# The head of a fused FNet and gMLP kernel: the first DFT block in row halves, hh straight from x

## The chip, the cores and the metric

The kernel runs on one core of a Trainium2 chip, in float32 (matmul operands in float32r). The metric is the device time of one execution in microseconds (us). The core's engines work side by side, each through its own queue in order: TensorE (PE, with its weight loads as PEld), VectorE (DVE), ScalarE (ACT), GpSimd (POOL), and SyncE (SP), which here issues transfers.

## The reference

```python
def _layernorm(x, axis=-1, eps=1e-5):
    m = jnp.mean(x, axis=axis, keepdims=True)
    v = jnp.var(x, axis=axis, keepdims=True)
    return (x - m) / jnp.sqrt(v + eps)

def _A_ref(x, dft_seq_re, dft_seq_im, dft_hid_re, dft_hid_im):
    a = jnp.einsum("bsd,ed->bse", x, dft_hid_re)
    b = jnp.einsum("bsd,ed->bse", x, dft_hid_im)
    return jnp.einsum("ts,bse->bte", dft_seq_re, a) - jnp.einsum("ts,bse->bte", dft_seq_im, b)

x = A_x                                       # (1, 2048, 512)
mod = (_silu(c) @ w_mod).reshape(1, 6, 1, -1)
sa, ca, ga, sb, cb, gb = (mod[:, i] for i in range(6))
h = _layernorm(x) * (1 + ca) + sa
x = x + ga * _A_ref(h, dft_seq_re, dft_seq_im, dft_hid_re, dft_hid_im)
h = _layernorm(x) * (1 + cb) + sb
x = x + gb * _B_ref(h, w_in, w_sp, b_sp, w_out)   # gMLP: GELU, layernorm, a 2048x2048 product, w_out
```

Only the first layernorm and the first product along the sequence, with the 2048x2048 matrices dft_seq_re and dft_seq_im, bear on this change.

## The kernel before

The kernel is one program written out in order. Its first part multiplies the normalized x with the DFT matrices of the sequence. The 2048 rows of x are cut into 16 tiles of 128 rows (s = 0 to 15), the matrices into blocks of 512x512. A step n is one tile s against 128 columns of one block: four of them make a block (k = 0 to 3), steps 0 to 3 are the block of dft_seq_re at the top left, steps 4 to 7 that of dft_seq_im.

Products keep float32 accuracy by splitting each operand: a high part (hh of the normalized tile, ah of the block, rounded to float32r by a copy on ScalarE) and a low part, the remainder (hl and al, a subtraction on VectorE). A step is then three groups of four matmuls, hh with ah, hh with al, hl with ah, one matmul for each quarter of the 512 hidden columns. In steps 0 to 3 (mm_a, n below 4) the three groups are issued one after the other, so that each needs its operands only when its turn comes.

A block arrives in `stage`, a tile of 128 partitions by 16 by 128: partition 32a + j holds the columns 128a to 128a + 127 of the rows 32b + j, b from 0 to 15. To feed a step, VectorE transposes it in squares of 32x32 (`squares`, "the turn"): turn k takes 32 columns of each group a, and all rows. load_block issues four transfers, one for each a. For block 0 it was called twice, on 64 of the 128 columns each time (`s0` to `s1`), so that the turns k = 0 and 1 need the first half, 2 and 3 the second.

The tiles of x: stats_first (rows 0 and 1) and stats_x (later ones) take mean and variance on VectorE and make scale and shift on POOL; norm_x writes the normalized tile xn on ScalarE, its column 0 being set to 1 by a memset (DFT's first hidden column is dealt with elsewhere); hi_h copies xn to hh, lo_h subtracts. prep_hi(n) turns and copies (t, ah), prep_lo(n) subtracts (al).

Order is set by the program's text: each engine runs its instructions in the order in which the calls stand at the end of the function; later work is hung on steps by `at(n, ...)`. Tiles have a fixed number of buffers (`stage` and `t` two, `ah` four, `al` three). The first transfers are issued on SP, those of x's second tile on ScalarE. While data is on its way, keep_busy issues filler matmuls of ones on TensorE:

```python
def keep_busy(n, k):
    ps = bank(k, "busyp")
    for _ in range(n):
        nc.tensor.matmul(ps, ones, busy, start=True, stop=True)
```

Of the kernel before, what the change touches and what calls it, by code (L numbers as in the profile page):

```python
# [8 lines left out]
F32 = mybir.dt.float32  # L9
F32R = mybir.dt.float32r  # L10
AF = mybir.ActivationFunctionType
ALU = mybir.AluOpType

P = 128
# [5 lines left out]
def fnet_gmlp_kernel(  # L20
# [32 lines left out]
    nc = tc.nc  # L53
# [3 lines left out]
    Q = 512  # L57
    NQ = S // Q
    NS = S // P
    ND = D // P  # L60
# [5 lines left out]
    def pool(name, side="left", bufs=1):  # L66
        return tc.tile_pool(name=name, bufs=bufs, side=side, reuse_waits="tile")
# [6 lines left out]
    blocks = ctx.enter_context(pool("blocks"))  # L74
# [4 lines left out]
    def bank(k, name):  # L79
        return psum.tile([P, 512], F32, tag=f"bank{k}", bufs=1, name=name)  # L80
# [30 lines left out]
    def norm(src, name):  # L111

        mean, rstd = stats(src, name)
        nmr = small.tile([P, 1], F32, tag="nmr" + name, name="nmr" + name)
        nc.gpsimd.tensor_scalar(nmr, mean, rstd, -1.0, op0=ALU.mult, op1=ALU.mult)
        return rstd, nmr
# [6 lines left out]
    def at(n, f, *a):  # L123
        fill.setdefault(n, []).append((f, a))
# [9 lines left out]
    src = []  # L134
# [15 lines left out]
    stage, T, AH, AL = {}, {}, {}, {}  # L150

    def load_block(tile_, a, s0=0, s1=P):
        v = a.rearrange("(b j) (a s) -> a j b s", j=32, a=4)
        for q in range(4):
            nc.sync.dma_start(tile_[32 * q:32 * q + 32, :, s0:s1], v[q][:, :, s0:s1])
# [9 lines left out]
    def load(b):  # L165
        if b < len(src):
            stage[b] = blocks.tile([P, 16, P], F32, tag="stage", bufs=2, name=f"stage{b}")
            load_block(stage[b], src[b])
        elif b < len(src) + 2:
            j = b - len(src)  # L170
            XB.append(blocks.tile([P, 4, Q], F32, tag="stage", bufs=2, name=f"xb{j}"))
            for g in range(2):
                nc.sync.dma_start(XB[j][:, 2 * g:2 * g + 2], ht_d[g].rearrange("(k p) t -> p k t", p=P)[:, 2 * j:2 * j + 2])
                for kk in range(2):
                    TT[2 * j + kk, g] = XB[j][:, 2 * g + kk]
        elif 4 * (b - NB0) < NE - N4:
            i, gh = divmod(b - NB0, NQ)
            g, h = divmod(gh, 2)
            p = PROD[i]
            stage[b] = blocks.tile([P, 2, 16, 64], F32, tag="stage", bufs=2, name=f"stage{b}")  # L180
            for r in range(2):
                load_half(stage[b][:, r], s_d[S_OF[p], r, g] if p in S_OF else
                          quad(w_sp, r + (2 if p == 4 else 0), g + (2 if p == 1 else 0)), h)
# [5 lines left out]
    def squares(dst, block, k):  # L189
        nc.vector.transpose(dst.rearrange("p (b i) -> p b i", i=32), block[:, :, 32 * k:32 * k + 32])  # L190
# [10 lines left out]
    def slot(i, name, dtype=F32):  # L201
        return slots[0].tile([P, Q], dtype, tag=f"slot{i}", bufs=1, name=name)
# [33 lines left out]
    def form_t(n):  # L236

        stage1 = n < N3
        p = (YPROD if stage1 else ZPROD)[(n - (N2 if stage1 else N3)) // 4]
        gg, kk = divmod(n % 4, 2)  # L240
        a, b, c, d = TT[kk, gg], TT[2 + kk, gg], TT.get((kk, 2 + gg)), TT.get((2 + kk, 2 + gg))
        if p == 6:
            if stage1:
                S2[gg, kk] = slot(13 + 2 * gg + kk, f"s2_{gg}{kk}")
                nc.vector.tensor_tensor(S2[gg, kk], d, XD[kk] if gg else c, op=ALU.subtract)
            return S2[gg, kk]
        if stage1:
            return {1: a, 2: b, 7: a, 4: b, 5: c, 3: d}[p]
        if p in (1, 2):
            t = blocks.tile([P, Q], F32, tag="t", bufs=2, name=f"t{n}")  # L250
            nc.vector.tensor_tensor(t, a if p == 1 else b, S2[gg, kk], op=ALU.subtract if p == 1 else ALU.add)
            return t
        return {7: c, 4: d, 5: a, 3: b}[p]
# [5 lines left out]
    highs, lows, SE = set(), set(), []  # L259
# [8 lines left out]
    def prep_hi(n):  # L268
        if n >= NE or n in highs:
            return  # L270
        highs.add(n)
        if N2 <= n < N4:
            T[n] = form_t(n)
        else:
            b, k = divmod(n, 4) if n < N2 else (NB0 + (n - N4) // 4, (n - N4) % 4)
            if b != NB0:
                T[n] = blocks.tile([P, Q], F32, tag="t", bufs=2, name=f"t{n}")
            if b == NB0:
                assert n in T
            elif n >= N4:  # L280
                squares(T[n], stage[b][:, k % 2], k // 2)
            else:
                squares(T[n], stage[b], k)
        AH[n] = SE[2][:, n - N4] if N4 <= n < N4 + 4 else blocks.tile([P, Q], F32R, tag="ah", bufs=4, name=f"ah{n}")
        nc.scalar.activation(AH[n], T[n], AF.Copy)  # L285
        if not N2 <= n < N4 and k == 3:
            stage.pop(b)
            if b != NB0:
                load(b + 2)


    def prep_lo(n):
        if n >= NE or n in lows:
            return
        lows.add(n)
        if N2 <= n < N4 and n % 4 == 3:
            AL[n] = slot(0, f"al{n}", F32R) if slots else zrow[0].tile([P, Q], F32R, tag="z1u", bufs=6, name=f"al{n}")
        elif N4 <= n < N4 + 4:
            AL[n] = slot(9 + n - N4, f"al{n}", F32R)
        else:  # L300
            AL[n] = blocks.tile([P, Q], F32R, tag="al", bufs=3, name=f"al{n}")
        t = T.pop(n)
        nc.vector.tensor_tensor(AL[n], t, AH[n].bitcast(F32), op=ALU.subtract)  # L303
        gg, kk = divmod(n % 4, 2)
        if NY[7] <= n < NY[7] + 4:
            nc.vector.tensor_tensor(TT[2 + kk, gg], TT[2 + kk, gg], S2[gg, kk], op=ALU.subtract)
# [6 lines left out]
    spool = s1.enter_context(pool("spool", "right"))  # L313
    GP_ = []
    hp = ctx.enter_context(ExitStack())
    hpool = hp.enter_context(pool("hpool"))
# [4 lines left out]
    ones = cpool.tile([P, P], F32, name="ones")  # L321
# [62 lines left out]
# [5 lines that stand above are left out]
# [14 lines left out]
    X, XG, LN, NRM, h_hi, h_lo = {}, {}, {}, {}, {}, {}  # L403
# [12 lines left out]
    def stats_x(s):  # L416
        NRM[s] = norm([X[s]], "x")

    def stats_first(s):

        m = spool.tile([P, 12], F32, tag="first", bufs=2, name=f"first{s}")
        nc.vector.bn_stats(m[:, :6], X[s])
        mv = m[:, 8:]
        nc.vector.bn_aggr(mv[:, :2], m[:, :6])
        nc.vector.tensor_scalar(mv[:, 1:2], mv[:, 1:2], EPS, None, op0=ALU.add)
        nc.gpsimd.tensor_tensor(mv[:, 2:3], mv[:, 1:2], mhalf, op=ALU.pow)
        nc.gpsimd.tensor_scalar(mv[:, 3:4], mv[:, 0:1], mv[:, 2:3], -1.0, op0=ALU.mult, op1=ALU.mult)
        NRM[s] = mv[:, 2:3], mv[:, 3:4]

    def sum_x(s):  # L430

        LN[s] = spool.tile([P, D], F32, tag="xn", bufs=4, name=f"xn{s}")
        m = NRM[s] = spool.tile([P, 4], F32, tag="sums", bufs=3, name=f"sums{s}")
        nc.scalar.activation(LN[s], X[s], AF.Copy, accum_out=m[:, 0:1])
        nc.gpsimd.tensor_scalar(m[:, 0:1], m[:, 0:1], -1.0 / D, 1.0, op0=ALU.mult, op1=ALU.mult)
# [21 lines left out]
    def hi_h(s):  # L457
        h_hi[s] = hpool.tile([P, ND, P], F32R, name=f"hh{s}")
        nc.scalar.activation(*parts_h(s, h_hi), AF.Copy)

    def lo_h(s):
        h_lo[s] = hpool.tile([P, ND, P], F32R, name=f"hl{s}")
        lo, h = parts_h(s, h_lo)
        nc.vector.tensor_tensor(lo, h, parts_h(s, h_hi)[0].bitcast(F32), op=ALU.subtract)
        LN.pop(s)
# [513 lines left out]
    load_x(0, range(1, 2), nc.scalar)  # L979
    nc.scalar.activation(sc, ones[:, :ND], AF.Silu)  # L980
    stage[0] = blocks.tile([P, 16, P], F32, tag="stage", bufs=2, name="stage0")
    load_block(stage[0], src[0], 0, P // 2)
    load_x(0, range(2, 4))
    load_block(stage[0], src[0], P // 2, P)
    load(1)
    load_x(1, range(2))
    keep_busy(5, 5)
    for s in range(2):
        LN[s] = spool.tile([P, D], F32, tag="xn", bufs=4, name=f"xn{s}")
        nc.gpsimd.memset(LN[s][:, 0:1], 1.0)  # L990
        stats_first(s)
    norm_x(0)
    hi_h(0)
    prep_hi(0)
    norm_x(1)
    lo_h(0)
    prep_lo(0)
    hi_h(1)
    prep_hi(1)
    stats_x(2)  # L1000
    lo_h(1)
    prep_lo(1)
    norm_x(2)
    prep_hi(2)
    stats_x(3)
    hi_h(2)
    norm_x(3)
    at(0, lo_h, 2)
    at(0, hi_h, 3)
    at(1, lo_h, 3)  # L1010
    at(0, load_x, 1, range(2, 4))
    at(2, load_row)
# [7 lines left out]
    for s, n in ((4, 4), (5, 4), (6, 6), (7, 6), (8, 10), (9, 10)):  # L1020
        m = n + (s == 9)
# [295 lines left out]
```

## Time and profile before

| what | us |
|---|---|
| median of three runs (lowest, highest) | 942.41 (942.01, 942.84) |
| the profiled execution | 942.69 |
| its span, first to last instruction | 940.9 |
| busy in the span: TensorE, VectorE, ScalarE, POOL | 932.1, 738.3, 413.6, 195.8 |
| first matmul of step 0 | 9.38 |
| first matmul of step 4 | 21.47 |

Rows of the timeline give start, length, engine, line, operation, output<-input, shapes and, in brackets, how long the engine had stood still and what ended it. Line numbers are those of the kernel before. "SPq" rows are issues of transfers, not their course. Rows of a group give its total and mean length and the idle time ahead of it.

### The profile page before, as it was taken

The page shows a single profiled execution, that of the slowest core. Times are in us where ns is not written, and L with a number is a line of the kernel's source. Part 1 is how long each engine was busy: PE and PEld are TensorE (multiplying, and loading weights), DVE is VectorE, ACT ScalarE, POOL GpSimd, SP SyncE. Part 2 cuts the span into 40 slices and gives each one's busy share as a digit, 9 for nine tenths or more (in the row PEclk, how much of TensorE's full clock was granted, in tenths as well). Part 3 has the DMA queues.
Part 4 walks back from the last instruction along what each step waited for, and adds up shares of the span by engine and source line. Part 5 has one row for each costly group of instructions (what it writes and reads, how often), then busy time and mean ns, then how long its engine had stood idle before and what let it go on. Part 6 is the DMA issues. An engine that isn't in the chain of part 4 may idle for free.

```text
span 940.9 us, 12362 instructions
## 1 busy us (share of the span) xinstructions
PE 932.1 (99%) x4114; PEld 772.7 (82%) x4114; DVE 738.3 (78%) x1201; ACT 413.6 (44%) x726; POOL 195.8 (21%) x372
## 2 busy tenths in 40 slices
PE   9999999999999999999989999999999999999998
PEld 5888888888888888888868999888888888888886
DVE  6899957778677677875888878899799889886662
ACT  4684424232132222222577678675545544331221
POOL 2330000114554165323414211332000000000000
PEclk9999999999999999999999999999999999999999
DMA  9994762647539977994777523344564466743541
GB/s 213 226 235 103 143 146 67 168 134 180 144 87 321 275 212 216 275 332 151 240 264 278 180 95 74 90 100 104 133 142 106 114 145 139 182 110 140 185 173 56
DMA packets 236592, 157.07 MB, mean 167 GB/s; under 512 B 131472, under 2 KB 203408, under 8 KB 236400
## 3 DMA queue, kind: packets, MB, share of 16 engines
q1 hardware_dynamic: 223008, 118.65, 50.5%
q0 software_dynamic: 12128, 37.11, 11.0%
q8 instruction: 32, 0.52, 0.2%
q10 hardware_dynamic: 1392, 0.52, 0.2%
q14 instruction: 32, 0.26, 0.1%
HBM read 119.54 MB, written 36.70 MB: 166 GB/s over the span
## 4 chain that ended last, share of the span: by engine, by line
PE 92%; DVE 2%; DMA 2%; ACT 1%; POOL 1%; issue 1%; SPq 1%; DVEq 0%; ACTq 0%; POOLq 0%
PE gp L95 12%; PE gp L96 12%; PE gp L97 12%; PE gw L97 10%; PE gw L96 10%; PE gw L95 10%; PE op L96 3%; PE op L95 3%; PE op L97 3%; PE yp L97 3%; PE yp L96 3%; PE yp L95 3%; PE z2p L97 2%; PE z2p L95 2%; PE z2p L96 2%; PE z1p L97 1%
## 5 line engine op out<-in xcount | busy, mean ns | idle before, releaser
L285 ACT ACTIVATE ah<-t 128x512 fp32r<-128x512 f32 x244 | 154.1, 632 | 369.7 <-DVE t L190 240.6
L303 DVE TENSOR_TENSOR al<-t,ah 128x512 fp32r<-128x512 f32 x244 | 164.5, 676 | 65.3 <-PE gp L96 38.8
L95 PE MATMUL gp<-ah,hh 128*128 128x512 f32 x496 | 192.9, 389 | 0.0
L96 PE MATMUL gp<-al,hh 128*128 128x512 f32 x496 | 192.9, 389 | 0.0
L97 PE MATMUL gp<-ah,hl 128*128 128x512 f32 x496 | 192.9, 389 | 0.0
L190 DVE STREAM_TRANSPOSE t<-stage 128x512 f32<-128x512 f32 x236 | 165.9, 703 | 6.9 <-DMA stage<-in_A_dft_seq_re_dram 3.0
L96 PE MATMUL gw<-al,bh 128*128 128x512 f32 x400 | 155.6, 389 | 0.0
L97 PE MATMUL gw<-ah,bl 128*128 128x512 f32 x384 | 149.5, 389 | 0.0
L95 PE MATMUL gw<-ah,bh 128*128 128x512 f32 x384 | 149.4, 389 | 0.0
L97 PEld LDWEIGHTS gp<-ah,hl 128*128 128x128 f32 x496 | 93.1, 188 | 19.4
L95 PEld LDWEIGHTS gp<-ah,hh 128*128 128x128 f32 x496 | 93.1, 188 | 19.4
L96 PEld LDWEIGHTS gp<-al,hh 128*128 128x128 f32 x496 | 93.1, 188 | 19.2
L96 PEld LDWEIGHTS gw<-al,bh 128*128 128x128 f32 x400 | 75.1, 188 | 15.7
L97 PEld LDWEIGHTS gw<-ah,bl 128*128 128x128 f32 x384 | 72.1, 188 | 15.0 <-DVE bl L852 0.3
L95 PEld LDWEIGHTS gw<-ah,bh 128*128 128x128 f32 x384 | 72.1, 188 | 15.0
L824 POOL DMA_DIRECT2D s_d<-sj x64 | 35.1, 548 | 103.8 <-DVE sj L816 80.2
L95 PE MATMUL yp<-hth,gh 128*128 128x512 f32 x128 | 49.8, 389 | 0.0
L96 PE MATMUL yp<-htl,gh 128*128 128x512 f32 x128 | 49.8, 389 | 0.0
L97 PE MATMUL yp<-hth,gl 128*128 128x512 f32 x128 | 49.8, 389 | 0.0
L605 POOL DMA_DIRECT2D ht_d<-hturn x62 | 40.9, 665 | 23.6 <-DVE hturn L601 19.6
L95 PE MATMUL op<-woh,uh 128*128 128x512 f32 x112 | 43.6, 389 | 0.0
L96 PE MATMUL op<-wol,uh 128*128 128x512 f32 x112 | 43.6, 389 | 0.0
(220 smaller groups left out, 1466.4 us busy)
## 6 DMA issues: line engine op xcount, KB each, us to landing
stage<-in_A_dft_seq_im_dram SPq DMA_DIRECT2D x64, 256.0 KB, 5.2
sj<-in_B_w_sp_dram SPq DMA_DIRECT2D x32, 512.0 KB, 7.6
s_d<-sj POOLq DMA_DIRECT2D x64, 256.0 KB, 4.1
stage<-s_d SPq DMA_DIRECT2D x128, 128.0 KB, 2.7
stage<-in_A_dft_seq_re_dram SPq DMA_DIRECT2D x60, 256.0 KB, 5.3
stage<-in_B_w_sp_dram SPq DMA_DIRECT2D x88, 128.0 KB, 3.0
wm<-in_w_mod_dram SPq DMA_DIRECT2D x16, 256.0 KB, 5.8
xr<-in_A_x_dram POOLq DMA_DIRECT2D x16, 256.0 KB, 4.6
```

The source lines that it names most:

```text
L95: nc.tensor.matmul(acc, ah, bh, start=first, stop=False, skip_group_check=go_on)
L96: nc.tensor.matmul(acc, ah, bl, start=False, stop=False, skip_group_check=go_on)
L97: nc.tensor.matmul(acc, al, bh, start=False, stop=last, skip_group_check=go_on)
L190: nc.vector.transpose(dst.rearrange("p (b i) -> p b i", i=32), block[:, :, 32 * k:32 * k + 32])
L285: nc.scalar.activation(AH[n], T[n], AF.Copy)
L303: nc.vector.tensor_tensor(AL[n], t, AH[n].bitcast(F32), op=ALU.subtract)
L605: eng.dma_start(v[a, i], ht[32 * a:32 * a + 32].rearrange("c (b r) -> c b r", r=32))
L824: nc.gpsimd.dma_start(s_d[m, r, g][b * P:(b + 1) * P, :], a)
```

## The change

It has three parts.

1. Block 0 is loaded in halves of its rows (load_rows): four transfers for b = 0 to 7, four for b = 8 to 15, each of 128 KB with contiguous runs of 128 floats (before 64 floats). Both halves are issued ahead of the tiles 2 and 3 of x, which had stood between the column halves.
2. Turn 0 and its ah are made in halves (half_first), 256 columns each. The other turns of the block are whole. al of step 0 is subtracted once for both.
3. hh of the tiles 0 to 3 is made straight from x (hi_first): one activation with scale and shift, and one that writes ones into column 0. xn is still made, for hl. All four tiles use stats_first, so `first` gets four buffers. In VectorE's order the second tile's statistics stand behind the first half turn, and xn of each tile behind hh on ScalarE; one filler matmul of five is left out.

```diff
+    def load_rows(j):
+        v = src[0].rearrange("(b j) (a s) -> a j b s", j=32, a=4)
+        for q in range(4):
+            nc.sync.dma_start(stage[0][32 * q:32 * q + 32, 8 * j:8 * j + 8], v[q][:, 8 * j:8 * j + 8])
+
+    def half_first(j):
+        if not j:
+            highs.add(0)
+            T[0] = blocks.tile([P, Q], F32, tag="t", bufs=2, name="t0")
+            AH[0] = blocks.tile([P, Q], F32R, tag="ah", bufs=4, name="ah0")
+        c = slice(Q // 2 * j, Q // 2 * (j + 1))
+        nc.vector.transpose(T[0][:, c].rearrange("p (b i) -> p b i", i=32), stage[0][:, 8 * j:8 * j + 8, :32])
+        nc.scalar.activation(AH[0][:, c], T[0][:, c], AF.Copy)
+
+    def hi_first(s):
+        h_hi[s] = hpool.tile([P, ND, P], F32R, name=f"hh{s}")
+        h = h_hi[s].rearrange("p k (a i) -> p k a i", i=32)
+        nc.scalar.activation(h, X[s].rearrange("p (a k i) -> p k a i", a=4, i=32), AF.Identity,
+                             bias=NRM[s][1], scale=NRM[s][0])
+        nc.scalar.activation(h_hi[s][:, 0, :1], ones[:, :1], AF.Copy)
...
-    load_block(stage[0], src[0], 0, P // 2)
+    load_rows(0)
+    load_rows(1)
     load_x(0, range(2, 4))
-    load_block(stage[0], src[0], P // 2, P)
     load(1)
     load_x(1, range(2))
-    keep_busy(5, 5)
+    keep_busy(4, 5)
...
-        stats_first(s)
+    stats_first(0)
+    half_first(0)
+    hi_first(0)
+    stats_first(1)
+    half_first(1)
+    prep_lo(0)
     norm_x(0)
-    hi_h(0)
-    prep_hi(0)
+    hi_first(1)
+    prep_hi(1)
+    lo_h(0)
+    prep_lo(1)
+    stats_first(2)
     norm_x(1)
-    lo_h(0)
-    prep_lo(0)
-    hi_h(1)
-    prep_hi(1)
-    stats_x(2)
+    prep_hi(2)
     lo_h(1)
-    prep_lo(1)
+    hi_first(2)
     norm_x(2)
-    prep_hi(2)
-    stats_x(3)
-    hi_h(2)
+    stats_first(3)
+    hi_first(3)
     norm_x(3)
     at(0, lo_h, 2)
-    at(0, hi_h, 3)
```

VectorE's queue from the first statistics to al of step 1, before. Here t_187 and t_198 are the turns of steps 0 and 1, hl_192 and hl_211 the low parts of tiles 0 and 1, bstx the statistics of tile 2:

```order
L422 BN_STATS first_170<-x_129 128x6
L422 BN_STATS first_178<-x_129 128x6
L190 STREAM_TRANSPOSE t_187<-stage_139 128x512
L464 TENSOR_TENSOR hl_192<-xn_168,hh_185 128x512
L303 TENSOR_TENSOR al_194<-t_187,ah_189 128x512
L190 STREAM_TRANSPOSE t_198<-stage_139 128x512
L103 BN_STATS bstx<-x_129 128x6
L464 TENSOR_TENSOR hl_211<-xn_176,hh_196 128x512
L303 TENSOR_TENSOR al_213<-t_198,ah_200 128x512
```

After. t_177 is the turn of step 0, t_198 and t_213 those of steps 1 and 2, first_206 the statistics of tile 2, first_225 of tile 3:

```order
L441 STREAM_TRANSPOSE t_177<-stage_139 128x256
L422 BN_STATS first_184<-x_129 128x6
L441 STREAM_TRANSPOSE t_177<-stage_139 128x256
L303 TENSOR_TENSOR al_192<-t_177,ah_178 128x512
L190 STREAM_TRANSPOSE t_198<-stage_139 128x512
L485 TENSOR_TENSOR hl_202<-xn_167,hh_181 128x512
L303 TENSOR_TENSOR al_204<-t_198,ah_200 128x512
L422 BN_STATS first_206<-x_129 128x6
L190 STREAM_TRANSPOSE t_213<-stage_139 128x512
L485 TENSOR_TENSOR hl_217<-xn_169,hh_195 128x512
L422 BN_STATS first_225<-x_129 128x6
L190 STREAM_TRANSPOSE t_238<-stage_139 128x512
```

The low part of tile 1 (hl_217) now stands behind the statistics of tile 2 and the turn of step 2, and the low parts of the blocks (al) ahead of those of the tiles.

ScalarE's queue for tiles 2 and 3, before (ah_220 and ah_239 are steps 2 and 3, hh_231 and hh_266 tiles 2 and 3):

```order
L119 ACTIVATE xn_215<-x_129,nmrx,rsx 128x511
L285 ACTIVATE ah_220<-t_218 128x512
L459 ACTIVATE hh_231<-xn_215 128x512
L119 ACTIVATE xn_233<-x_129,nmrx,rsx 128x511
L285 ACTIVATE ah_239<-t_237 128x512
L459 ACTIVATE hh_266<-xn_233 128x512
```

After (ah_215 and ah_240 are steps 2 and 3, hh_219 and hh_231 tiles 2 and 3):

```order
L285 ACTIVATE ah_215<-t_213 128x512
L447 ACTIVATE hh_219<-x_129,first_206 128x512
L449 ACTIVATE hh_219<-ones 128x1
L119 ACTIVATE xn_222<-x_129,first_206 128x511
L447 ACTIVATE hh_231<-x_129,first_225 128x512
L449 ACTIVATE hh_231<-ones 128x1
L119 ACTIVATE xn_234<-x_129,first_225 128x511
L285 ACTIVATE ah_240<-t_238 128x512
```

ah of step 3 now stands behind hh and xn of tile 3.

More of the change, by code (lines that the diff above doesn't have):

```diff
@@ L419, in stats_first @@
     def stats_first(s):
-        m = spool.tile([P, 12], F32, tag="first", bufs=2, name=f"first{s}")
+        m = spool.tile([P, 12], F32, tag="first", bufs=4, name=f"first{s}")
         nc.vector.bn_stats(m[:, :6], X[s])
```

## The prediction

> **What bounds the kernel now.** I read the page's head first, then the windows by stage, then TensorE's own timeline at the start, and last the other engines there.
>
> ```profile
> span 940.9 us, 12362 instructions
> PE 932.1 (99%) x4114; PEld 772.7 (82%) x4114; DVE 738.3 (78%) x1201; ACT 413.6 (44%) x726; POOL 195.8 (21%) x372
> ```
>
> ```profile
> 9.38:21.25 11.87, 11.41 (x48) 8.78 (x48) 9.78 (x19) 6.90 (x11) 3.31 (x8) 1.00 1.15 237
> 21.25:35.00 13.75, 13.75 (x62) 11.41 (x61) 12.43 (x23) 8.64 (x14) 5.25 (x16) 1.00 1.15 221
> 200.00:930.00 730.00, 727.55 (x3241) 607.67 (x3240) 581.93 (x942) 316.92 (x547) 163.39 (x278) 1.00 0.59 170
> ```
>
> In a window's row the first pair is its length and TensorE's busy time. From 21.25 us on TensorE is busy without a gap, and between 200 and 930 us it rests only 2.45 us. So a time at which TensorE gets through its first four steps is carried to the end of the program almost whole. Those steps, n = 0 to 3, are the 48 matmuls that stand between 9.38 and 21.47 us:
>
> ```profile
> 1.53 7.60 PE L388 MATMUL busyp<-busy,ones 128*128 128x512 f32 x10 [1.53 <-DVE busy L327]
> 9.38 1.20 PE L483 MATMUL gp<-ah,hh 128*128 128x512 f32 x4 [0.25 <-ACT ah L285]
> 10.42 1.08 PE L483 MATMUL gp<-al,hh 128*128 128x512 f32 x4
> 11.34 1.08 PE L483 MATMUL gp<-ah,hl 128*128 128x512 f32 x4
> 15.37 1.20 PE L483 MATMUL gp<-ah,hh 128*128 128x512 f32 x4 [0.24 <-ACT hh L459]
> 21.47 0.39 PE L95 MATMUL gp<-ah,hh 128*128 128x512 f32 x1
> ```
>
> Each step is three groups of four. A group takes 0.92 us from start to start (10.42 to 11.34), or 1.04 when TensorE had stood still (9.38 to 10.42). The four steps take 12.09 us. The number to forecast is where 21.47 goes.
>
> **What feeds those steps.** Start, length and wait of the others:
>
> ```profile
> 3.88 0.20 ACT L980 ACTIVATE sc<-ones 128x4 f32<-128x4 f32 x1
> 4.92 0.69 DVE L422 BATCH_NORM_STATS2 first<-x 128x6 f32<-128x512 f32 x1 [3.53 <-DMA x<-in_A_x_dram]
> 5.86 0.15 DVE L425 TENSOR_SCALAR first<-first 128x1 f32<-128x1 f32 x1
> 6.83 0.27 POOL L427 TENSOR_SCALAR first<-first 128x1 f32<-128x1 f32 x1
> 7.13 0.81 ACT L119 ACTIVATE xn<-x,first 128x511 f32<-128x511 f32 x1 [3.04 <-POOL xn L990]
> 7.95 0.71 DVE L190 STREAM_TRANSPOSE t<-stage 128x512 f32<-128x512 f32 x1 [0.82 <-DMA stage<-in_A_dft_seq_re_dram]
> 8.70 0.63 ACT L285 ACTIVATE ah<-t 128x512 fp32r<-128x512 f32 x1
> 9.36 0.69 DVE L303 TENSOR_TENSOR al<-t,ah 128x512 fp32r<-128x512 f32 x1
> 9.97 0.70 DVE L190 STREAM_TRANSPOSE t<-stage 128x512 f32<-128x512 f32 x1
> 13.46 0.82 ACT L119 ACTIVATE xn<-x,nmrx,rsx 128x511 f32<-128x511 f32 x1 [2.12 <-POOL xn L450]
> 14.19 0.62 ACT L285 ACTIVATE ah<-t 128x512 fp32r<-128x512 f32 x1
> 14.71 0.62 ACT L459 ACTIVATE hh<-xn 128x512 fp32r<-128x512 f32 x1
> 14.77 0.68 DVE L190 STREAM_TRANSPOSE t<-stage 128x512 f32<-128x512 f32 x1
> ```
>
> The first transpose waits for the block; ah ends at 9.33 and TensorE starts at 9.38. An instruction that needs nothing from its forerunner starts before that one's end: 0.61 us after the start of a 0.69 one on VectorE (9.36 to 9.97), 0.73 and 0.52 on ScalarE (13.46, 14.19, 14.71). Statistics take 1.09 us on VectorE (4.92 to 6.01) and again 1.09 until POOL's scale and shift are there (7.10). Later POOL is slower:
>
> ```profile
> L108 POOL TENSOR_TENSOR rsx<-mvx,mhalf 128x1 f32<-128x1 f32 x8 | 5.4, 670 | 0.7
> L115 POOL TENSOR_SCALAR nmrx<-mvx,rsx 128x1 f32<-128x1 f32 x8 | 2.7, 333 | 0.8
> ```
>
> With these means and the gaps seen at 6 us (0.25) it is about 1.3.
>
> **The transfers.** Before, step 0 needs only the first column half of the block, four transfers of 128 KB. After, its transpose needs both row halves, eight transfers, since a square of 32 columns runs through all rows. Their slots on SP's queue are those of rows 3.15 and 5.35:
>
> ```profile
> 3.15 2.15 SPq L155 DMA_DIRECT2D stage<-in_A_dft_seq_re_dram  x4
> 5.35 1.90 SPq L412 DMA_DIRECT2D x<-in_A_x_dram  x4
> 7.29 2.02 SPq L155 DMA_DIRECT2D stage<-in_A_dft_seq_re_dram  x4
> ```
>
> From issue to landing the last transfers of these three rows took:
>
> ```profile
> stage<-in_A_dft_seq_re_dram SPq DMA_DIRECT2D x1, 128.0 KB, 3.0
> ...
> x<-in_A_x_dram SPq DMA_DIRECT2D x1, 128.0 KB, 3.2
> ...
> stage<-in_A_dft_seq_re_dram SPq DMA_DIRECT2D x1, 128.0 KB, 4.4
> ```
>
> and the shortest of all in this block is the first number here:
>
> ```profile
> DMA to landing us min/median/max: 2.1/5.3/6.9
> ```
>
> The eighth transfer is issued at about 6.7 (its slot today begins at 6.8; issues of x, with fewer runs, are a little shorter). I take 3.0, the row of the same tile, size and queue depth: landing at 9.7. The bounds are 2.1 and 4.4, 8.8 to 11.1.
>
> ```profile
> 4.00:6.00 2.00, 2.00 (x4) 0.74 (x3) 1.02 (x3) 0.09 (x1) 0.00 (x0) 1.00 0.70 161
> 7.00:9.00 2.00, 2.00 (x4) 0.55 (x3) 1.14 (x3) 1.75 (x3) 0.95 (x4) 1.00 0.93 236
> ```
>
> The last column is GB/s: the stretch in which mostly column halves (runs of 256 B) moved has 161, the one with x in it 236. The Trainium skill ("DMA: Bandwidth & Descriptors", Specifications) asks for at least 512 B per run for full rate; the row halves have just that. By that rule the first 0.52 MB would take 2.2 us and not 3.3 us, and the landing would come up to 1.0 us sooner, and the sum below would be +0.8 in place of +1.8. The low bound of 8.8 has that in it from the rows alone.
>
> **The steps of the change, summed.** Half a transpose: between 0.36 (half of 0.71) and 0.71; I take 0.40. Half of ah: 0.20 (the 128x4 row) plus half of the rest of 0.63, 0.41. hh from x is an activation with scale and shift like the 0.81 row, in place of a 0.63 copy, and writing its first column anew is a 0.20 row: each hh costs ScalarE about 0.3 us more. In return hh does not wait for xn.
>
> - Start. Landed 9.7; second half turned 9.8 to 10.2; second half of ah 10.25 to 10.65; TensorE 10.7 against 9.38: +1.3. The first halves (turned at about 7.8) and hh of row 0 (done by 9.5) lie beside the transfers and cost nothing; the second row's statistics, now queued behind the first half turn, end by 9.3 and are covered too.
> - Step 0. al follows ah, ready at 11.4 and needed at 11.75; hl, behind the next turn and xn, 12.6, needed at 12.65. No wait, but no slack: step 1 begins at 13.55.
> - Step 1. ah at 12.8 and al at 13.5 are in time. hl stands behind statistics of row 2 and turn 2: 13.4 + 1.1, turn to 15.15, hl 15.05 to 15.7. Needed at 15.4: a wait of 0.35 with restart, step 2 could begin at 16.8.
> - Step 2. hh of row 2: statistics 14.5 + 1.3 = 15.8, then 0.81 and 0.20: 16.85. Start 16.9. al stands behind row 3's statistics and turn 3 and is ready at 17.95: wait 0.15. TensorE free at 19.95.
> - Step 3. ScalarE has hh and xn of row 3 ahead of ah: statistics 16.7 + 1.3 = 18.0, hh with column 18.1 to 19.1, xn to 19.8, ah 19.7 to 20.35. Start 20.4, wait 0.45. Then 1.04 + 0.92 + 0.92: step 4 at 23.25.
>
> The same steps took 12.09 us and take 12.55. Sum: +1.3 at the start, +0.45 in waits, **+1.8 us** at 21.47. The block loaded in the freed buffer (issued once turn 3 is done, at about 17.4 where row 14.77 ends at 15.45) comes 2 us later, as TensorE does; the window after 21.25 shows no wait that this would touch. The fifth filler matmul that is left out ends before the data in both cases and gains nothing.
>
> The profiled execution took 942.69 us, 1.8 around its span; it becomes 944.5. The median of the runs, 942.41, is 0.28 lower: **944.2 us**. 0.2% of it, 1.9 us, is about what a measurement tells from no change, and the forecast stands at that edge.
>
> **Rivals.**
>
> *TensorE's clock falls while it waits* (slower). Filler rows and the program's end:
>
> ```profile
> 6.79 0.34 PEld L388 LDWEIGHTS busyp<-busy,ones 128*128 128x128 f32 x1 [0.52 <-issue]
> 8.11 0.19 PEld L388 LDWEIGHTS busyp<-busy,ones 128*128 128x128 f32 x1 [0.24 <-issue]
> ```
>
> ```profile
> 936.80:937.00 0.20, 0.03 (x1) 0.00 (x0) 0.06 (x1) 0.00 (x0) 0.00 (x0) 1.00 0.00 0
> 939.40:939.60 0.20, 0.00 (x0) 0.00 (x0) 0.00 (x0) 0.00 (x0) 0.00 (x0) 0.91 0.00 0
> ```
>
> The fillers' loads ran at 0.34, then at 0.19: TensorE was slow for its first 6 us. At the end the granted clock (third number from the right) falls 2.7 us after the last matmul. With four fillers the last ends at about 8.2 (9.13 less two passes, of which two follow the load at 8.11, some 0.45 each), and TensorE stands for 2.5 us until 10.7: it decides from about 2.7 on, that is from a landing at 9.9 on. Six microseconds at 0.19/0.34 of the speed lose 2.6, of which the waits of steps 1 to 3 cover 0.95: +1.7 more, 945.9. For it: the two lengths nearly meet. Against it: 2.5 is below 2.7. The Trainium skill ("TensorE: Matmul & The Clock Gate", Part 1) lets the clock fall after an idle window of about 3.4 us that runs freely; by that rule 2.5 us is too short, but the trace's fall after 2.7 us shows that less than a full idle window can do.
>
> *Early landing and no waits* (not slower). With a landing after 2.1 us TensorE starts at 9.8, and 48 matmuls without a wait take 11.05 (48 at 0.23): step 4 at 20.85, 0.6 earlier, 941.8. It decides from a landing before 9.4 with hl of step 1 and ah of step 3 in time. For it: hh no longer waits for xn, and turns 2 and 3 wait for no transfer, as the row half holds all columns. Against: the two waits come from order on VectorE and ScalarE, not from transfers, and shift with the start.
>
> *The delay is absorbed later.* The 2.45 us of rest after 200 us could take the 1.8 up: 942.4. Against: what TensorE waits for there is made from its own results, so it shifts as well.
>
> **How the numbers follow.** Forecast case 0.62; its own range is +0.5 (landing 8.8, POOL at 1.09) to +3.5 (landing 11.1), so a little more than half of it lies beyond 1.9: 0.33 slower, 0.29 same. Clock 0.20, all slower. Early landing 0.10 (0.09 same, 0.01 faster), absorbed 0.08 (0.07 same, 0.01 faster). Together 0.53 slower, 0.45 same, 0.02 faster. The range for 8 in 10 runs from +0.4 to +3.7 on the median, which leaves out the early landing and the tail of the clock's case: 942.8 to 946.1.
>
> **What the profile after would show.** The first real matmul at 10.7 (start), waits of TensorE on DVE before the third group of step 1 and on ACT before step 3, step 4 at 23.25, busy without a gap from there. Wrong, if the first matmul stands before 10 us, if loads of 0.34 show after 10 us (clock), or if step 4 begins at 21.5 or before.

## The result, and the profile after

| what | before | after |
|---|---|---|
| median, us (lowest to highest, runs) | 942.82 (942.01 to 943.90, 7) | 945.88 (945.38 to 946.23, 7) |
| the profiled execution | 942.69 | 945.53 |
| its span | 940.9 | 943.7 |
| first matmul of step 0 | 9.38 | 10.97 |
| first matmul of step 4 | 21.47 | 24.10 |

The change makes the kernel slower: after over before is 1.0033, 95% interval 1.0022 to 1.0043, or 3.06 us between the medians. The forecast was 944.2 with a range of 942.8 to 946.1, so the side is right and the time lies inside, near the upper end. One execution of all those timed below, at 1169.98 us with a mean granted clock of 0.754, is far slower than the others of its kernel and is left out of the ratios.

The page of the changed kernel begins:

```profile
span 943.7 us, 12360 instructions
PE 931.0 (99%) x4112; PEld 773.1 (82%) x4112; DVE 738.7 (78%) x1204; ACT 414.9 (44%) x731; POOL 196.4 (21%) x370
```

Windows of the changed kernel: the first four steps, what follows, and the main part (length, TensorE's busy time and count, then weight loads, VectorE, ScalarE and POOL, the granted clock, the DMA share, GB/s):

```profile
9.38:21.25 11.87, 10.06 (x37) 7.88 (x37) 8.55 (x18) 8.00 (x16) 3.41 (x8) 0.86 1.03 209
24.00:35.00 11.00, 11.00 (x51) 9.09 (x50) 10.79 (x21) 6.52 (x11) 5.25 (x16) 1.00 1.12 223
200.00:930.00 730.00, 727.30 (x3239) 607.46 (x3238) 580.54 (x940) 315.86 (x546) 163.42 (x278) 1.00 0.60 171
```

After step 4 little differs: TensorE is busy without a gap from 24 us to 200 us, and its rest between 200 and 930 us is 2.70 us, 0.25 more than before. So the loss is made in the head, and two numbers hold it: step 0 starts 1.59 us later, and steps 0 to 3 take 13.13 us in place of 12.09 (+1.04). Together that is the 2.63 us by which step 4 is late. The granted clock of the first window is new, 0.86 where it was 1.00.

TensorE's timeline there, changed kernel (start, length, and in brackets the idle time and what ended it):

```profile
1.53 5.24 PE L388 MATMUL busyp<-busy,ones 128*128 128x512 f32 x8 [1.53 <-DVE busy L327]
10.97 1.63 PE L504 MATMUL gp<-ah,hh 128*128 128x512 f32 x4 [4.20 <-ACT ah L442]
...
15.41 1.07 PE L504 MATMUL gp<-ah,hh 128*128 128x512 f32 x4
...
21.23 1.20 PE L504 MATMUL gp<-ah,hh 128*128 128x512 f32 x4 [0.22 <-ACT ah L285]
...
24.10 0.39 PE L95 MATMUL gp<-ah,hh 128*128 128x512 f32 x1
```

Two things show. The fillers end at 6.77 and TensorE then stands for 4.20 us; step 0 takes 4.44 us (10.97 to 15.41) where 2.85 were forecast (10.7 to 13.55). And step 3 waits for its ah (ScalarE) until 21.23, though TensorE was through step 2 at about 20.85. Windows of 1 us of TensorE (length, busy, granted clock, DMA share, GB/s) say why step 0 is long:

```profile
11.00:12.00 1.00, 1.00 (x4) 0.76 1.05 217
12.00:13.00 1.00, 1.00 (x4) 0.50 1.23 225
...
14.00:15.00 1.00, 1.00 (x4) 0.53 1.26 228
15.00:16.00 1.00, 1.00 (x6) 1.00 1.22 214
```

The clock falls to 0.50 at about 11.5 us, after TensorE's long rest, and is back at about 15. The start comes from this chain on VectorE and ScalarE:

```profile
10.03 0.45 DVE L441 STREAM_TRANSPOSE t<-stage 128x256 f32<-128x256 f32 x1 [1.00 <-DMA stage<-in_A_dft_seq_re_dram]
10.51 0.42 ACT L442 ACTIVATE ah<-t 128x256 fp32r<-128x256 f32 x1 [1.07 <-DVE t L441]
```

And the late ah of step 3 from this one on VectorE, POOL and ScalarE:

```profile
16.87 0.15 DVE L425 TENSOR_SCALAR first<-first 128x1 f32<-128x1 f32 x1
17.11 0.55 POOL L426 TENSOR_TENSOR first<-first,mhalf 128x1 f32<-128x1 f32 x1 [0.93 <-DVE first L425]
17.57 0.65 DVE L303 TENSOR_TENSOR al<-t,ah 128x512 fp32r<-128x512 f32 x1
17.75 1.11 POOL L427 TENSOR_SCALAR first<-first 128x1 f32<-128x1 f32 x1
18.14 0.68 DVE L485 TENSOR_TENSOR hl<-xn,hh 128x512 fp32r<-128x512 f32 x1
18.90 0.82 ACT L447 ACTIVATE hh<-x,first 128x512 fp32r<-128x512 f32 x1 [0.96 <-POOL xn L471]
20.56 1.13 ACT L285 ACTIVATE ah<-t 128x512 fp32r<-128x512 f32 x2
```

The statistics of tile 3 were forecast to be ready at 16.7 on VectorE and 1.3 us later on POOL. They leave VectorE at 17.02, and POOL needs until 18.86: its shift, 0.27 us long earlier in the head, takes 1.11, and it ends 0.04 us after the second of two VectorE subtractions that run beside it. The row of ah holds two; the first (0.61 us) is step 3's and ends at 21.17.

Two theories stand after this. *Order*: the queue of ScalarE, with POOL's slow shift ahead of it, sets step 3, and the fall of the clock is hidden behind that. *Clock*: the fall sets step 3, and the order costs little.

### The profile page after: what moved, and what is told of

Its sections match the earlier page's. It is cut to its first block, busy times and chain, and to the rows that moved or that the text cites. A ratio compares the mean times of both kernels' runs of the same rounds, so it can differ in the third digit from the quotient of the medians.

```text
span 943.7 us, 12360 instructions
## 1 busy us (share of the span) xinstructions
PE 931.0 (99%) x4112; PEld 773.1 (82%) x4112; DVE 738.7 (78%) x1204; ACT 414.9 (44%) x731; POOL 196.4 (21%) x370
## 4 chain that ended last, share of the span: by engine, by line
PE 92%; DVE 3%; ACT 2%; DMA 1%; POOL 1%; issue 1%; SPq 0%; DVEq 0%; ACTq 0%; POOLq 0%
PE gp L95 12%; PE gp L96 12%; PE gp L97 12%; PE gw L97 10%; PE gw L95 10%; PE gw L96 10%; PE op L96 3%; PE op L95 3%; PE op L97 3%; PE yp L96 3%; PE yp L95 2%; PE yp L97 2%; PE z2p L95 2%; PE z2p L96 2%; PE z2p L97 2%; PE z1p L97 1%
## 5 line engine op out<-in xcount | busy, mean ns | idle before, releaser
L95 PE MATMUL gp<-ah,hh 128*128 128x512 f32 x496 | 193.0, 389 | 0.0
L95 PE MATMUL gw<-ah,bh 128*128 128x512 f32 x384 | 149.4, 389 | 0.0
L95 PEld LDWEIGHTS gp<-ah,hh 128*128 128x128 f32 x496 | 93.1, 188 | 19.4
L95 PEld LDWEIGHTS gw<-ah,bh 128*128 128x128 f32 x384 | 72.1, 188 | 14.9
L95 PE MATMUL yp<-hth,gh 128*128 128x512 f32 x128 | 49.8, 389 | 0.0
L95 PE MATMUL op<-woh,uh 128*128 128x512 f32 x112 | 43.6, 389 | 0.0
```

Of the source, the lines that this page charges most:

```text
L95: nc.tensor.matmul(acc, ah, bh, start=first, stop=False, skip_group_check=go_on)
```

## The experiments

Each was timed in five rounds beside the kernel before, which had a median of 942.55 in the first four, 942.50 in the next four and 942.67 in the last three. Line numbers of TensorE's helper move with the edits (L483 to L510); "step 3" is the row of ah,hh that begins it, "step 4" the first row of L95. The mean granted clock of an execution tells, to about 0.001, whether the clock fell, for runs without a profile too: a fall to half speed for 3.4 us takes 0.002 off the mean over 943 us, one of 6.8 us takes 0.004. (The profiled execution before, without a fall in its head, reads 0.999.)

**The changed kernel again.**

> The changed kernel once more, as the base of the next three. Both theories: 945.9, that is 3 us above the kernel before; first matmul at about 11, step 4 at about 24.1.

Measured: 945.71 (945.23 to 945.79), ratio 1.0034 (1.0021 to 1.0046). Its profile is not that of the first one, though the time is:

```profile
11.02 2.07 PE L504 MATMUL gp<-ah,hh 128*128 128x512 f32 x4 [3.48 <-ACT ah L442]
...
21.84 1.07 PE L504 MATMUL gp<-ah,hh 128*128 128x512 f32 x4
...
24.56 0.39 PE L95 MATMUL gp<-ah,hh 128*128 128x512 f32 x1
```

```profile
9.00:10.00 1.00, 0.00 (x0) 0.82 0.96 228
...
16.00:17.00 1.00, 1.00 (x5) 0.77 1.10 243
```

The windows are of 1 us as before. With a clock that is either 1.0 or 0.5, their means put the fall at 9.64 and the return at 16.46. All of step 0 ran at half speed, and step 3 begins with no wait for ah, which was ready at about 21.2 as in the first profile. TensorE reached step 3 at 20.85 there and at 21.84 here. So in one execution of the same program ScalarE's queue ends last, in another the slow TensorE. The mean clocks fit: 0.998 in the first profiled execution, with the clock down from 11.52 to 14.94, and 0.996 in this one. One of the five runs has a mean of 1.0, and it still took 945.23.

**Seven fillers**, so that TensorE hardly rests before step 0.

```diff
-    keep_busy(4, 5)
+    keep_busy(7, 5)
```

> Seven filler matmuls in place of four, so that TensorE hardly stands still before step 0. Order theory (the end of the four steps is set by ah of step 3, which stands behind hh and xn of tile 3 on ScalarE and was ready at 21.2, while TensorE was free at 20.85 even with the slow clock): the clock stays up, step 0 takes 2.9 us and not 4.4, TensorE then waits longer before step 3, step 4 stays at 24.1 and the time at 945.9, within 0.3. Clock theory (the slow clock costs its 1.6 us): step 4 at 22.5 and 944.3.

Measured: 945.52 (945.32 to 945.89), ratio 1.0033 (1.0021 to 1.0045). The clock did not fall in the profiled execution, and nothing was won:

```profile
11.25 1.20 PE L504 MATMUL gp<-ah,hh 128*128 128x512 f32 x4 [0.57 <-ACT ah L442]
...
15.11 1.07 PE L504 MATMUL gp<-al,hh 128*128 128x512 f32 x4
16.35 1.21 PE L504 MATMUL gp<-ah,hl 128*128 128x512 f32 x4 [0.17 <-DVE hl L485]
...
21.51 1.19 PE L504 MATMUL gp<-ah,hh 128*128 128x512 f32 x4 [0.86 <-ACT ah L285]
...
24.37 0.39 PE L95 MATMUL gp<-ah,hh 128*128 128x512 f32 x1
```

Both waits of the forecast now stand in the profile: the third group of step 1 waits for hl, and step 3 for ah. This is the theory of the order. Taken alone it would have closed the case wrongly, as the next runs show.

**ah of step 3 ahead of hh of tile 3** on ScalarE.

```diff
     stats_first(3)
+    prep_hi(3)
     hi_first(3)
```

> Turn and ah of step 3 put ahead of hh and xn of tile 3, four fillers as in the change. Order theory: the wait before step 3 goes, step 3 starts when TensorE is free, 20.85, where the clock fell: step 4 at 23.6, 0.5 us less, 945.4; in executions in which the clock did not fall, up to 1.3 less. Clock theory: also 0.5 less, so this run alone does not tell them apart.

Measured: 946.09 (945.36 to 946.66), ratio 1.0038 (1.0026 to 1.0051): a miss, nothing is won here either. ah was in time, but the clock was at half from about 9.4 to 16.3 us and TensorE came to step 3 no sooner:

```profile
21.84 1.07 PE L504 MATMUL gp<-ah,hh 128*128 128x512 f32 x4
```

**Both edits together.**

> Seven fillers and ah of step 3 first. Order theory: neither cover is left, step 3 starts behind hh of tile 3 at about 20, step 4 at 22.8, 1.3 us less than the changed kernel: 944.6, much more than the sum of the two edits taken apart (0 and 0.5). Clock theory: 1.6 + 0.5 less, 943.8, the plain sum of the two.

Measured: 944.33 (943.88 to 945.18 in ten runs, and the one of 1169.98), ratio 1.0019 (1.0010 to 1.0028), 1.4 us below the changed kernel, where the edits alone gave 0.2 and -0.4.

```profile
11.04 1.20 PE L504 MATMUL gp<-ah,hh 128*128 128x512 f32 x4 [1.70 <-ACT ah L442]
...
20.28 1.10 PE L504 MATMUL gp<-ah,hh 128*128 128x512 f32 x4
```

Steps 0 to 3 take 12.01 us (11.04 to step 4 at 23.05), as long as before the change, and the start alone is late, by 1.66 against the 9.38 of the profile before. The time above the kernel before is 1.78. So the 3 us fall into a late start that costs 1.8 and some 1.3 more. Of these the order alone costs 1.2 (seven fillers, 945.52), and the fall alone at least as much (ah first, 946.09, where four of the five runs have a mean clock of 0.996); they do not add.

**The row halves alone**: kernel before, with load_rows and half_first for step 0, x as before.

```diff
...
-    load_block(stage[0], src[0], 0, P // 2)
+    load_rows(0)
+    load_rows(1)
     load_x(0, range(2, 4))
-    load_block(stage[0], src[0], P // 2, P)
...
-        stats_first(s)
+    stats_first(0)
+    half_first(0)
+    stats_first(1)
     norm_x(0)
     hi_h(0)
-    prep_hi(0)
+    half_first(1)
```

> The kernel before with the block loaded in row halves and turn and ah of step 0 in halves; hh made from xn as before, five fillers. Order theory: start at 11.0 (+1.6), hh of tile 2 at about 17.5 and of tile 3 at about 20 still behind POOL's three small steps, step 4 at 23.3: +1.8 on the kernel before, 944.6. Rival (the late start is the whole cost): +1.6 and no waits beyond those of before: 944.4, the waits before steps 2 and 3 gone.

Measured: 944.99 (944.04 to 945.52), ratio 1.0024 (1.0015 to 1.0033). Four of its ten runs have a mean granted clock of 1.0 and took 944.04 to 944.64, the six at 0.998 took 944.99 to 945.52. Without the fall it is thus the 944.4 that was expected if the late start is the whole cost (944.6 with the order's waits, too near to tell apart), and the fall costs about 0.8 here:

```profile
11.31 2.07 PE L497 MATMUL gp<-ah,hh 128*128 128x512 f32 x4 [3.82 <-ACT ah L442]
```

**hh from x alone**: the changed kernel with the block in column halves again and turn 0 whole.

```diff
-    load_rows(0)
-    load_rows(1)
+    load_block(stage[0], src[0], 0, P // 2)
     load_x(0, range(2, 4))
+    load_block(stage[0], src[0], P // 2, P)
...
     stats_first(0)
-    half_first(0)
     hi_first(0)
     stats_first(1)
-    half_first(1)
+    prep_hi(0)
     prep_lo(0)
```

> The changed kernel with the block loaded in column halves as before and step 0 turned whole; hh from x and the changed order of the queues stay, four fillers. Order theory: first matmul at 9.4, no slow clock, but waits before the third group of step 1 (0.6) and before step 3 (0.8, ah behind hh and xn): step 4 at 22.3, +0.8, 943.6. Rival (all of the loss is the row halves): step 4 at 21.4 or earlier, 942.8 or less.

Measured: 944.40 (943.73 to 944.81), ratio 1.0018 (1.0009 to 1.0027), 0.8 above what was expected. TensorE, and three windows:

```profile
9.82 1.97 PE L504 MATMUL gp<-ah,hh 128*128 128x512 f32 x4 [2.12 <-ACT ah L285]
```

```profile
18.78 1.07 PE L504 MATMUL gp<-ah,hl 128*128 128x512 f32 x4
20.19 1.20 PE L504 MATMUL gp<-ah,hh 128*128 128x512 f32 x4 [0.34 <-ACT ah L285]
```

```profile
9.50:10.00 0.50, 0.18 (x1) 0.96 1.19 253
10.00:10.50 0.50, 0.50 (x2) 0.50 1.16 236
13.00:14.00 1.00, 1.00 (x5) 0.81 1.17 211
```

The clock fell at about 9.96, after a rest of only 2.12 us and just as TensorE had begun again, and was back 3.4 us later. ah of step 3 is late here too: step 3 could have followed at 19.70 (18.78, the last group of step 2, and 0.92). The new order costs by itself, without the row halves. The seven runs with a mean clock of 0.999 or more took 943.73 to 944.58 (median 944.08), the four at 0.998 took 944.40 to 944.81. So 1.6 of the 1.9 above the kernel before is there without the fall, and the wait for ah, which the order sets, is the only one that the profile shows within the four steps.

**No fillers**: the kernel before without its five.

```diff
-    keep_busy(5, 5)
```

> The kernel before without filler matmuls: the price of a slow TensorE by itself. Steps 0 and 1 run at about 0.42 us a matmul for 3.4 to 6.8 us: 1.5 to 3 us lost, of which the waits before steps 2 and 3 (0.8 with their restarts) cover that much: +0.7 to +2.2, 943.5 to 945.0. If the fillers do nothing here, no change.

Measured: 943.61 (943.00 to 944.54), ratio 1.0014 (1.0005 to 1.0022), inside what was expected.

```profile
9.71 2.08 PE L483 MATMUL gp<-ah,hh 128*128 128x512 f32 x4 [9.71 <-ACT ah L285]
11.59 1.80 PE L483 MATMUL gp<-al,hh 128*128 128x512 f32 x4
13.23 1.09 PE L483 MATMUL gp<-ah,hl 128*128 128x512 f32 x4
```

A TensorE that starts slow loses 0.84 and 0.72 us in the first two groups (1.88 and 1.64 between starts, 1.04 and 0.92 at speed), 1.56 together, and step 4 comes at 22.33, 0.86 later than in the profile before: the waits that the old order has later take some of it up. The granted clock in the windows of these 4 us reads 1.00, so that column does not show the slow start of a program; it shows a fall later on.

**hh from x for tiles 2 and 3 alone**, on the kernel before, with ah of step 3 ahead of hh of tile 3 and al of step 3 ahead of the next block's turn.

```diff
...
-    stats_x(2)
+    stats_first(2)
     lo_h(1)
     prep_lo(1)
-    norm_x(2)
+    hi_first(2)
     prep_hi(2)
-    stats_x(3)
-    hi_h(2)
+    norm_x(2)
+    stats_first(3)
+    prep_hi(3)
+    hi_first(3)
     norm_x(3)
     at(0, lo_h, 2)
-    at(0, hi_h, 3)
+    at(0, prep_lo, 3)
```

> The kernel before with hh from x for tiles 2 and 3 alone, ah of step 3 ahead of hh of tile 3, al of step 3 ahead of the next block's turn; loads as before. Order theory: the waits before steps 2 and 3 (with restarts 0.9) go, step 4 at 20.6, 0.9 us less than before, 941.9. Rival: hh from x only costs ScalarE time: no change or slower.

Measured: 942.00 (941.40 to 943.70), ratio 0.9993 (0.9984 to 1.0002). TensorE goes through its four steps without a wait, in 11.16 us where it took 12.09:

```profile
9.05 1.20 PE L490 MATMUL gp<-ah,hh 128*128 128x512 f32 x4 [1.56 <-ACT ah L285]
...
20.21 0.39 PE L95 MATMUL gp<-ah,hh 128*128 128x512 f32 x1
```

The same kernel once more:

> The same kernel as the run with hh straight from x for tiles 2 and 3 alone, once more, to narrow its interval: 942.0, 0.5 below the kernel before, if the gain at step 4 (20.21 against 21.47) is kept in part; 942.5 if that run was chance.

Measured: 942.16 (941.70 to 942.78), ratio 0.9993 (0.9984 to 1.0002). The four steps take 11.20 us again. Its profiled execution was the longest of the eleven, 942.78 with a span of 941.0, and TensorE's waits after 200 us show one that the other profiles lack:

```profile
PE gw L97 <- DVE bl L859: 1.0, 1, 1.0
```

**The same with six fillers:**

```diff
-    keep_busy(5, 5)
+    keep_busy(6, 5)
```

> The last kernel with six fillers instead of five. If the spread of its times (941.4 to 943.7) is the clock falling in the idle time before the first matmul: no times above 942.3, median 941.9. If the fillers run slowly until 7.6 us, six of them end near 10 us and delay the first matmul by up to 0.9 us: median 942.4 to 942.8. If neither matters: 942.0.

Measured: 942.15 (941.87 to 942.33), ratio 0.9993 (0.9984 to 1.0002). No time is above 942.33, as the clock's theory wants, but the median does not move: in its profile the fillers end at 9.86, by an end that the profile models, and step 0 starts right behind them at 9.79, 0.7 later than in the two profiles with five. All three series lie 0.5 below the kernel before, and each interval still holds 1.0. That this part alone makes the kernel faster is likely and not shown, and why only 0.5 of the 0.9 saved in the head arrives is open, but for the one wait above.

**POOL's shift of tile 3 on ScalarE**, with seven fillers. VectorE negates the mean, POOL only takes the power, ScalarE multiplies.

```diff
-        nc.gpsimd.tensor_scalar(mv[:, 3:4], mv[:, 0:1], mv[:, 2:3], -1.0, op0=ALU.mult, op1=ALU.mult)
+        if s == 3:
+            nc.vector.tensor_scalar(mv[:, 0:1], mv[:, 0:1], -1.0, None, op0=ALU.mult)
+            SHIFT.append(lambda: nc.scalar.activation(mv[:, 3:4], mv[:, 0:1], AF.Copy, scale=mv[:, 2:3]))
+        else:
+            nc.gpsimd.tensor_scalar(mv[:, 3:4], mv[:, 0:1], mv[:, 2:3], -1.0, op0=ALU.mult, op1=ALU.mult)
...
-    keep_busy(4, 5)
+    keep_busy(7, 5)
...
     stats_first(3)
+    SHIFT[0]()
     hi_first(3)
```

> The changed kernel with seven fillers (so that the clock does not fall) and with the shift of the last tile (minus mean times factor) made on ScalarE instead of POOL; POOL keeps only the power. If POOL's shift, 1.11 us against 0.27 us elsewhere, is what makes hh of the last tile late: hh of that tile starts 0.7 to 0.8 us earlier than in the run with seven fillers (19.19 there), step 3 starts at about 20.7 instead of 21.51, step 4 at about 23.5 instead of 24.37, median 944.7. If POOL's shift does not hold it (another wait takes its place, on VectorE or in ScalarE's queue): step 3 at 21.5 and 945.5, as with seven fillers alone.

Measured: 945.07 (944.38 to 945.79), ratio 1.0024 (1.0014 to 1.0033). The profile does what the theory of POOL says:

```profile
17.77 0.28 ACT L429 ACTIVATE first<-first 128x1 f32<-128x1 f32 x1
18.09 0.82 ACT L453 ACTIVATE hh<-x,first 128x512 fp32r<-128x512 f32 x1
...
19.75 1.14 ACT L285 ACTIVATE ah<-t 128x512 fp32r<-128x512 f32 x2
```

```profile
10.90 1.20 PE L510 MATMUL gp<-ah,hh 128*128 128x512 f32 x4 [0.28 <-ACT ah L448]
...
20.42 1.20 PE L510 MATMUL gp<-ah,hh 128*128 128x512 f32 x4
...
23.28 0.39 PE L95 MATMUL gp<-ah,hh 128*128 128x512 f32 x1
```

From the start of step 0 to that of step 4 it is 12.38 us, against 13.12 with seven fillers alone: the expected 0.7. The time of this execution is 944.38, and the three runs with a clock of 1.0 lie at 944.38 to 944.49, 1.1 below the run with seven fillers, of which 0.35 is the earlier start (10.90 against 11.25). The other six, at 0.998 to 0.999, took 945.03 to 945.79; they set the median. That the clock fell there is read from the mean clock alone, since none of them was profiled.

## Why the prediction was right, and where its sizes were not

- **The start.** Forecast 10.7; measured 10.97, and 10.90 to 11.31 in the six other profiles with row halves. The mechanism is the one forecast: the first turn needs the whole block, and the chain behind it is the half turn and half of ah. The mis-sized terms are the landing and the half turn. The eighth transfer, issued at about 6.7, took the length in the next row, so it landed at about 9.9 and not at 9.7, and VectorE began at 10.03; the half turn took 0.45, not 0.40.

```profile
stage<-in_A_dft_seq_re_dram SPq DMA_DIRECT2D x2, 128.0 KB, 3.2
```

  The longer contiguous runs brought the transfers in hardly sooner: in the fourth place, where a column half took 3.0 us, row halves took 2.7 to 3.3 in seven profiles, and in the eighth 3.0 to 3.6. The rule of the Trainium skill on runs of 512 B ("DMA: Bandwidth & Descriptors", Specifications), by which the prediction estimated a landing up to 1.0 us earlier, is not borne out at this place.
- **Where the start of the unchanged chain lies.** The 9.38 of the one profile before was taken as fixed. With the same loads and the same first turn it was 9.05, 9.11, 9.71 and (hh from x alone) 9.82 in other profiles. A difference of two profiles at this place is good to some 0.4 us; the runs give 1.78 for the start (both edits together).
- **Step 1 waits for hl (0.35), step 2 for al (0.15).** Not seen in the profile after, since the slow step 0 covered them. With the clock kept, the third group of step 1 begins 0.32 late (15.11 + 0.92 = 16.03, seen 16.35): the term was right. Step 2's al is in time: it ends at 18.50, and its group begins at 18.61, 1.04 behind the first. Step 2 itself begins 0.18 late there (17.57 for 17.39), behind hh of tile 2; the sum had 0.1 at this place.
- **Step 3 waits for ah (0.45).** The wait is there; its size is the term that failed, "statistics 16.7 + POOL 1.3". POOL needed 1.84 (17.02 to 18.86). With the clock kept, ah came 10.21 us after the start of step 0 (20.85 + 0.61 less 11.25) where 9.65 had been forecast (20.35 less 10.7), and step 3 lost 1.0. The shift moved to ScalarE gave 0.7 of that back, which shows POOL's step as the cause. The forecast priced the shift by the mean of eight rows, 0.333 us. Seven of them are of 0.27, and the one long one stands in this very place, tile 3, beside two subtractions (15.37 to 16.62):

```profile
15.87 0.80 POOL L115 TENSOR_SCALAR nmrx<-mvx,rsx 128x1 f32<-128x1 f32 x1
```

- **"One filler fewer gains nothing", and the rest of 2.5 us.** Forecast: the last filler ends at 8.2. It ended at 6.77, and at 7.4 to 7.7 in three other profiles with four fillers: the moment at which TensorE comes to speed varies between executions (weight loads of 0.19 us from 4.89 on in the profile after, from 8.11 in the one before), and with it the end of the fillers. The rest before step 0 was 3.5 to 4.2 us with four fillers and row halves, and the clock fell.
- **The rival of the clock** (0.20, 945.9) therefore happened, and its time is almost the measured one. The sign that the forecast had named against itself came too: weight loads of 0.33 us each after 10 us, four in the next row.

```profile
11.97 1.61 PEld L504 LDWEIGHTS gp<-al,hh 128*128 128x128 f32 x4
```

  The agreement of the times is no proof of the rival: it let the fall add 1.7 to the forecast, and with the fall avoided the time was the same, 945.5. From the start of step 0 to that of step 3 it is 9.24 us with both edits. The order makes this 1.0 longer (10.26, seven fillers), the fall makes TensorE free 0.6 and 1.6 later (9.88 and 10.82 in the two profiles of the changed kernel). The two run side by side, and only with both gone does the time drop. The threshold of 2.7 us of rest was wrong as well: 2.12 us did it (hh from x alone), and the fall came anywhere from 2.1 us (7.53 to 9.64, the second profile of the changed kernel) to 4.8 us (6.77 to 11.52, the first) after the last filler. The Trainium skill ("TensorE: Matmul & The Clock Gate", Part 1) gives an idle window of about 3.4 us that runs freely; a rest of 2.12 us is shorter than that, so here the measurement decides; the way back, 3.4 us in that run, agrees with its busy window.
- **Early landing, and absorbed later.** Neither came: no start lay before 10.9, and the late start passed whole into the time (with both edits step 4 is 1.58 later and the time 1.78 longer). What was absorbed is the clock's fall, by the wait for ah.
- **The sum.** Forecast +1.3 and +0.45; measured +1.59 and +1.04 in the profile after, +1.64 and +1.45 in its repeat. Both terms were too small by the sizes above, and with them the forecast stood at the edge of what can be measured while the result lies clearly beyond it. That the change is slower, by a late start and a late ah, was forecast for the right reason. That the time still lies inside the range is in part luck: the main case held no fall of the clock, the fall came, and it cost little because the wait for ah, itself under-priced, covered it.

## What to carry to other kernels

Where two bounds lie close, an experiment that takes away one alone shows nothing and seems to acquit it: take both away, and then each alone, before you call either harmless. Cut a first load along the axis that lets the first consumer begin with a part; here half the columns fed a whole step, half the rows fed none. A wait moved ahead in an in-order queue must be priced with the longest length that its producer shows beside the same neighbours, not with its mean.

## What the runs showed of the hardware

- POOL's tiny shift (128x1) takes 0.27 us alone, 0.60 beside one VectorE subtraction and 1.11 beside two in a row, and ends within 0.15 us of the subtraction's end (16.15 and 16.02, 18.86 and 18.82 in the profile after). The Trainium skill ("SBUF — State Buffer", "SBUF: two separate sides") describes an exclusive lock of a port pair that such a VectorE operation and one of POOL share; the lengths agree with it, but no run changed the lock alone.
- Before step 0 the clock fell in every profile with a rest of 2.1 us or more behind the fillers and in none with 1.7 or less, and stayed down for 3.4 us in some executions (11.5 to 14.9 in the first profile of the changed kernel) and for 6.8 in others (9.64 to 16.46 in the second).
- The fillers' speed is a matter of the execution: eight passes took 5.24 to 6.16 us, fourteen 7.81 to 9.15, so seven fillers, which left a rest of 0.28 us in one execution, left 1.70 in another.
